# First mixture of experts: blocks beyond the second nested one inside the other, expert 0's third block without a condition, its redo inside the innermost condition

## The chip, the core and the metric

The kernel runs on one core of a Trainium2 chip. The metric is the device time of one execution in microseconds (us). Below, PE is TensorE, ACT ScalarE, DVE VectorE, POOL GpSimd and SP SyncE, which here only issues DMAs. Each engine has a sequencer of its own that reads its instruction stream, branches included.

## The reference, cut to what matters

Attention over chunks of 64 tokens gives 2304 rows of 512 values. A gate sends each row to one of 8 experts (the first mixture); a second mixture, dense over all 8 experts, follows and takes most of the time. The change is in the first mixture.

```python
logits = x @ w_gate
expert_idx = np.argmax(logits, axis=1)
...
h = np.maximum(np.einsum('ecd,edf->ecf', disp, w1), 0.0)
y = np.einsum('ecf,efd->ecd', h, w2)
...
out[i] = gate_w[i] * y[expert_idx[i], pos[i]]
```

With the inputs of the reference the experts 0 to 7 get 512, 128, 466, 384, 174, 128, 320 and 192 rows. This decides which conditional blocks run.

## The kernel before

Every matrix product is made of float16 high and low parts, so a product of weights and rows takes three matmul passes. For each expert of the first mixture the function `blocks` computes rows in blocks of 128: the first product (lines L346 for matmuls, ACT L351 and DVE L352 for what leaves PSUM as `hh` and `hl`), then for each 128 rows the second product `y` (L855, 24 matmuls of 512 columns), its scaling (ACT L860 and L866, DVE L867 and L873) and two writes to DRAM issued by SP (L870, L875).

The order of instructions on each engine is the order in which the code is written. Per expert it is: the first 256 rows always ("main"), with the weights of the next expert split into halves (`w_split`, L241 to L250) and statistics of the weights after those (L170, L172) written between its parts; then the rest under conditions on `rc`, the expert's row count, which every engine loads into a register (L909). `If(rc > 256)` is L992, `If(rc > 384)` is L993, and `If(rc > 512)` is L995. Above 384, rows 256 to 511 are computed as one block of 256; between 257 and 384 an `Else` computes a single block of 128; above 512 a loop (L996) takes further blocks.

So experts 0 and 2 run the block of 256, experts 3 and 6 the `Else`, and experts 1, 4, 5 and 7 skip everything from L992.

Expert 0 begins before routing is complete: its first 256 rows are taken when only a part of the rows has been routed. `e_count` holds how many rows expert 0 had by then. If these were at most 255, its first two blocks must be done again with the full list: that is the redo, L1010, behind a load of `e_count` (L1009). Here the count is 256, so the redo is skipped. `prep` is a list of statistics and one weight split that expert 0's conditional part carries; `later` is the list of loads of expert 3's weights, which SP issues (L159) after it.

PSUM is handed out in turn by name: "p" has three banks, "y" two, "c" two. Main takes "p" for first products and "y" for `y`; the conditional part takes "c" for both.

## Time and profile before

| what | value |
|---|---|
| device time, median of 3 runs | 1786.7 us (1784.45 to 1787.1) |
| the profiled execution, its own time | 1790.8 us |
| its span, first to last instruction | 1789.1 us |
| PE busy | 1704.3 us, 95% of the span |
| DVE, ACT, POOL busy | 67%, 54%, 41% |
| mean granted PE clock | 0.982 |
| first mixture, from expert 0's first matmul to the last row written | about 137 to 419 us of the span |

PE is busy nearly all the time, so what counts is where PE stands still, and why. In a timeline row, the bracket at the end gives the idle time before it and what ended it: an engine with its line, "PEq" for PE's own sequencer, or "issue" where nothing in the records explains the wait. Records whose engine ends in q are a sequencer's; COMPARE_BRANCH is a branch, with the time that it took.

### The profile page before, as it was taken

What the parts mean: (1) busy time and instruction counts of PE and PEld (TensorE: products, weight loads), DVE (VectorE), ACT (ScalarE), POOL (GpSimd) and SP (SyncE); (2) the same over time, 40 slices, a digit from 0 to 9 for tenths busy, and PEclk for the clock granted to TensorE, in tenths of its full rate; (3) what the DMA queues carried; (4) which work ended last, traced back from release to release, by engine and by line L of the source; (5) the groups of instructions that cost most, each with busy time, mean ns of one, the idle gap of its engine ahead of it and who ended that gap; (6) DMA issues with size and microseconds to landing.
All of it is one profiled execution on the core that took longest, in us unless ns stands there. A gap on an engine that the chain in (4) does not pass through costs nothing.

```text
span 1789.1 us, 33018 instructions
## 1 busy us (share of the span) xinstructions
PE 1704.3 (95%) x13011; PEld 1233.6 (69%) x13011; DVE 1196.4 (67%) x2347; ACT 958.8 (54%) x1814; POOL 731.4 (41%) x754
## 2 busy tenths in 40 slices
PE   7879899898999999999999999999999999999995
PEld 6766557565555477777777777777777777777774
DVE  4896556755467766686677667677766786676652
ACT  7866456665345455665365445555643665453440
POOL 1355435551121335453355245453534553443432
PEclk9989899999999999999999999999999999999998
DMA  9756678953524222332324224223323141231200
GB/s 236 205 168 174 181 194 177 234 131 97 145 65 168 104 104 83 110 137 76 130 63 171 95 77 161 97 100 109 128 86 130 62 171 71 101 125 63 97 37 36
DMA packets 140908, 219.22 MB, mean 123 GB/s; under 512 B 62880, under 2 KB 81392, under 8 KB 140720
## 3 DMA queue, kind: packets, MB, share of 16 engines
q1 hardware_dynamic: 133728, 198.92, 35.7%
q0 software_dynamic: 5360, 17.24, 3.4%
q8 instruction: 117, 1.92, 0.5%
q14 instruction: 71, 0.58, 0.1%
q10 hardware_dynamic: 1632, 0.56, 0.1%
HBM read 167.56 MB, written 41.91 MB: 117 GB/s over the span
## 4 chain that ended last, share of the span: by engine, by line
PE 68%; DVE 5%; ACT 2%; DMA 1%; issue 0%; POOLq 0%; ACTq 0%; DVEq 0%
PE p_m L1228 35%; PE p_m L1316 28%; PE p_m L1360 5%; DVE wall L292 3%; DVE acc L1295 1%; ACT wall L291 1%; DMA out_dram<-acc,rk 1%; DVE el L1236 0%; PE p_m L1116 0%; ACT eh L1233 0%; DMA x_d<-row 0%; DVE tq L1243 0%; ACT tq L1268 0%; DVE tq L1246 0%; DVE wall L250 0%
## 5 line engine op out<-in xcount | busy, mean ns | idle before, releaser
L1228 PE MATMUL p_m<-x,wall 128*128 128x384 f16 x4032 | 667.5, 326 | 6.9 <-ACT tq L1268 4.1
L1316 PE MATMUL p_m<-wall,eh 128*128 128x256 f16 x3528 | 580.3, 273 | 0.0
L1228 PEld LDWEIGHTS <-wall 128*128 128x128 f16 x4032 | 394.2, 98 | 264.7 <-issue 10.3
L1240 POOL TENSOR_TENSOR el<-tq,eh 128x384 f16<-128x384 f32 x336 | 344.5, 1053 | 558.4 <-ACT eh L1233 558.0
L1316 PE MATMUL p_m<-wall,el 128*128 128x256 f16 x1764 | 480.8, 273 | 0.3 <-DVE el L1236 0.3
L1233 ACT ACTIVATE eh<-tq 128x384 f16<-128x384 f32 x540 | 273.9, 522 | 190.5 <-DVE tq L1246 101.9
L1316 PEld LDWEIGHTS <-eh 128*128 128x128 f16 x3528 | 344.3, 98 | 44.3
L1295 DVE SCALAR_TENSOR_TENSOR acc<-p_m,cf,acc 128x256 f32<-128x256 f32 (+1 forms) x378 | 175.0, 520 | 128.1 <-PE p_m L1316 128.1
L1243 DVE TENSOR_TENSOR tq<-p_m,tq 128x384 f32<-128x384 f32 x288 | 158.3, 555 | 129.6 <-PE p_m L1228 128.6
L1316 PEld LDWEIGHTS <-el 128*128 128x128 f16 x1764 | 172.6, 98 | 20.6 <-DVE el L1236 0.6
L1236 DVE SCALAR_TENSOR_TENSOR el<-tq,eh 128x384 f16<-128x384 f32 x204 | 175.5, 862 | 10.0 <-ACT eh L1233 8.6
L1246 DVE SCALAR_TENSOR_TENSOR tq<-tq 128x384 f32<-128x384 f32 x252 | 133.0, 553 | 2.9
L346 PEld LDWEIGHTS <-wall 128*128 128x128 f16 x1152 | 107.2, 101 | 39.9 <-issue 23.1
L1268 ACT COPY tq<-p_m 128x384 f32<-128x384 f32 x96 | 45.6, 475 | 112.4 <-PE p_m L1228 110.1
L346 PE MATMUL p_p<-xT,wall 128*128 128x256 f16 x672 | 78.1, 277 | 15.7 <-PEq L1010 8.0
L1360 PE MATMUL p_m<-wall,eh 128*128 128x512 f16 x288 | 85.6, 379 | 0.0
L270 POOL TENSOR_TENSOR tq<-stb 128x256 f32<-128x256 f32 x56 | 48.9, 874 | 81.9 <-DVE wsumsq L186 58.9
L1281 ACT ACTIVATE tq<-tq 128x384 f32<-128x384 f32 x84 | 43.9, 523 | 70.1 <-DVE tq L1243 70.1
L291 ACT ACTIVATE wall<-stb,wsb 128x256 f16<-128x256 f32 (+1 forms) x56 | 31.3, 606 | 86.3 <-DMA wb_d<-wall 60.8
L242 POOL TENSOR_SCALAR stb<-stb,wsb 128x1024 f32<-128x1024 f32 x16 | 51.6, 3225 | 59.4 <-DVE tq L1243 47.2
L270 POOL TENSOR_TENSOR tq<-sta 128x256 f32<-128x256 f32 x56 | 45.0, 803 | 72.8 <-DVE wall L292 43.4
L292 DVE SCALAR_TENSOR_TENSOR wall<-stb,wsb,wall 128x256 f16<-128x256 f32 (+1 forms) x56 | 38.1, 689 | 50.2 <-ACT wall L291 47.4
(276 smaller groups left out, 2145.4 us busy)
## 6 DMA issues: line engine op xcount, KB each, us to landing
x<-xt_d SPq DMA_DIRECT2D x147, 384.0 KB
sta<-in_moe_w_dram SPq DMA_DIRECT2D x18, 1024.0 KB
stb<-in_moe_w_dram SPq DMA_DIRECT2D x18, 1024.0 KB
wb_d<-wall SPq DMA_DIRECT2D x20, 896.0 KB
wall<-wb_d SPq DMA_DIRECT2D x20, 896.0 KB
sta<-in_moe_w_dram SPq DMA_DIRECT2D x28, 512.0 KB
stb<-in_moe_w_dram SPq DMA_DIRECT2D x28, 512.0 KB
xt_d<-x SPq DMA_DIRECT2D x21, 384.0 KB
```

The costliest lines, as they stand in the source:

```text
L270: nc.gpsimd.tensor_tensor(out=at(o), in0=at(u), in1=at(v), op=op)
L292: nc.vector.scalar_tensor_tensor(out=o[:, cs, 1], in0=src, scalar=m.s, in1=o[:, cs, 0], op0=ALU.mult, op1=ALU.subtract)
L346: nc.tensor.matmul(p[:, f4, :], lhsT=w[:, kk, f * 128:(f + 1) * 128], rhs=xT[:, lo + kk, 0:W], start=(n == 0), stop=(n == 3 * KD - 1))
L1228: nc.tensor.matmul(p, lhsT=wt[:, w, lw, kk, :], rhs=xt[:, lx, kk, :], start=first and n == 0, stop=n == 5, skip_group_check=not first)
L1233: nc.scalar.activation(out=hs[op][0][:, q, :], in_=src, func=AF.Relu if op in (A11, A12, A22) or plain else AF.Copy)
L1236: nc.vector.scalar_tensor_tensor(out=hs[op][1][:, q, :], in0=src, scalar=0.0, in1=hs[op][0][:, q, :], op0=ALU.max, op1=ALU.subtract)
L1240: nc.gpsimd.tensor_tensor(out=hs[op][1][:, q, :], in0=src, in1=hs[op][0][:, q, :], op=ALU.subtract)
L1243: nc.vector.tensor_tensor(out=o, in0=a, in1=b, op=ALU.add)
L1246: nc.vector.scalar_tensor_tensor(out=o, in0=a, scalar=0.0, in1=b, op0=ALU.max, op1=op)
L1295: nc.vector.scalar_tensor_tensor(out=acc[:, j, cols], in0=y, scalar=coefs[x][:, j:j + 1], in1=acc[:, j, cols], op0=ALU.mult, op1=ALU.add)
L1316: nc.tensor.matmul(bk.t[:, cols], lhsT=hs[op][lh][:, q, t * 128:(t + 1) * 128], rhs=b.q[q][:, w, lw, :], start=m in (1, 5) and q == 0 and ...
L1360: nc.tensor.matmul(y.t, lhsT=h[:, kk % 4, c * 128:(c + 1) * 128], rhs=w[:, kk, :], start=(n == 0), stop=(n == 3 * KF - 1))
```

## The change

Expert 0's third block (`further(2)`) is computed without a condition, and holds `prep` in three parts where it was four. For the other experts it stands under `If(rc > 256)`, now L1017. Inside stands `If(rc > 384)`, L1020, with the fourth block (`further(3)`), and inside that `If(rc > 512)`, L1022, with `rest`: the loop, and for expert 0 the redo (L1008). So rows 256 to 511 are two single blocks, and there is no `Else`. For expert 0 `rc` is a new number, `e_more`: its count, or 2304 if the redo is due, so that the redo is reached. `y` in the nested blocks takes the banks "y"; what `rest` computes takes "c".

```diff
         def counted():
             nc.vector.tensor_copy(e_count, p_tab[:, 256:258])
+            nc.vector.tensor_scalar(out=e_redo, in0=p_tab[:, 256:257], scalar1=255.0, scalar2=float(N),
+                                    op0=ALU.is_le, op1=ALU.mult)
...
         nc.vector.tensor_copy(reg_i[:, 0:2 * E], p_tab[:, 256:256 + 2 * E])
+        nc.vector.tensor_tensor(out=e_more, in0=e_redo, in1=p_tab[:, 256:257], op=ALU.max)
...
-                y = bank("y", [128, DM])
+                y = in_turn(y_bank, [128, DM], F32, "p_y")
...
-                rc = count()
+                rc = count(True)
...
-            with tc.If(rc > 256) as more:
-                with tc.If(rc > 384) as cmp:
-                    blocks(x, (late_t, late_r), 2, ranks(2), [prep[0:4], prep[4:8], prep[8:], [], [], []])
+            def further(t, sites=()):
+                blocks(x, (late_t[:, :, (t - 2) * 128:(t - 1) * 128], late_r[t - 2:t - 1]), 1, lambda _: rank(t), sites)
+
+            def rest():
+                c = count() if x == 0 else rc
+                with tc.If(c > 512) if x == 0 else nullcontext():
+                    with tc.For_i(4, (c + 127) // 128, 1) as t:
...
+                if x == 0:
+                    with tc.If(nc.values_load(e_count[0:1, 0:1], min_val=0, max_val=N) <= 255):
+                        for t in range(2):
+                            blocks(x, turn(gather(tokens(0, t), "xgl", 1), "xTl", "c"), 1, lambda _, t=t: ranks(0)(t), y_bank="c")
...
+            if x == 0:
+                further(2, [prep[0:4], prep[4:], []])
+            with tc.If(rc > 256) if x > 0 else nullcontext():
+                if x > 0:
+                    further(2)
+                with tc.If(rc > 384):
+                    further(3)
                     with tc.If(rc > 512):
...
-                with cmp.Else():
-                    blocks(x, (late_t, late_r[:1]), 1, ranks(2), [prep[0:4], prep[4:], []])
+                        rest()
             if x == 0:
-                with more.Else():
-                    for f in prep:
-                        f()
-                known = nc.values_load(e_count[0:1, 0:1], min_val=0, max_val=N)
-                with tc.If(known <= 255):
-                    for t in range(2):
-                        blocks(x, turn(gather(tokens(0, t), "xgl", 1), "xTl", "c"), 1, lambda _, t=t: ranks(0)(t))
                 for f in later:
                     f()
```

On PE, this is what stands at the end of expert 0 before the change: from the last matmul of the conditional part to the first matmul of expert 1. The left-out rows are the two redo blocks.

```order
L855 MATMUL p_y<-wall,hl 128x512
L993 UNCONDITIONAL_BRANCH
L992 UNCONDITIONAL_BRANCH
L1009 TENSOR_LOAD e_count
L1010 COMPARE_AND_BRANCH
L331 LDWEIGHTS xg
...
L855 MATMUL p_y<-wall,hl 128x512
L1010 UNCONDITIONAL_BRANCH x2
L346 LDWEIGHTS wall
```

The same place on PE after the change, from the last matmul of the fourth block; the left-out rows are the loop's block and the two redo blocks.

```order
L860 MATMUL p_y<-wall,hl 128x512
L1022 COMPARE_AND_BRANCH
L914 TENSOR_LOAD reg_i
L1002 COMPARE_AND_BRANCH
...
L1008 TENSOR_LOAD e_count
L1008 COMPARE_AND_BRANCH
...
L860 MATMUL p_y<-wall,hl 128x512
L1008 UNCONDITIONAL_BRANCH x2
L1022 UNCONDITIONAL_BRANCH
L1020 UNCONDITIONAL_BRANCH
L348 LDWEIGHTS wall
```

The load of `e_count` and the branch on it no longer stand between the last block and expert 1: they lie in what L1022 jumps over, which holds the loop's block (258 instructions on PE) and the redo (512).

On DVE, expert 0's third and fourth block before the change, from the register load on (`stb`, `wsb` belong to the weights of the next experts):

```order
L909 TENSOR_LOAD reg_i
L992 COMPARE_AND_BRANCH
L993 COMPARE_AND_BRANCH
L352 SCALAR_TENSOR_TENSOR hl<-p_p,hh 128x512
L172 TENSOR_REDUCE wmxb<-stb_2263 128x1 x2
L352 SCALAR_TENSOR_TENSOR hl<-p_p,hh 128x512
L172 TENSOR_REDUCE wmxb<-stb_2263 128x1 x2
L352 SCALAR_TENSOR_TENSOR hl<-p_p,hh 128x512
L250 SCALAR_TENSOR_TENSOR w_3_2226<-stb_1830,wsb,w_2_2225 128x1024
L352 SCALAR_TENSOR_TENSOR hl<-p_p,hh 128x512
L89 TENSOR_SCALAR x2h<-ssq_2571 128x1
```

And after the change:

```order
L914 TENSOR_LOAD e_more
L354 SCALAR_TENSOR_TENSOR hl<-p_p,hh 128x4x128
L172 TENSOR_REDUCE wmxb<-stb_2267 128x1 x2
L354 SCALAR_TENSOR_TENSOR hl<-p_p,hh 128x4x128
L172 TENSOR_REDUCE wmxb<-stb_2267 128x1 x2
L250 SCALAR_TENSOR_TENSOR w_3_2230<-stb_1832,wsb,w_2_2229 128x1024
L89 TENSOR_SCALAR x2h<-ssq_2565 128x1
L872 SCALAR_TENSOR_TENSOR row_2573<-p_y,x2s,row_2573 128x2x256
L878 SCALAR_TENSOR_TENSOR rkt<-xg,x2i,iw 128x1
L1020 COMPARE_AND_BRANCH
L354 SCALAR_TENSOR_TENSOR hl<-p_p,hh 128x4x128 x2
```

All statistics and the split of `prep` now lie in the third block; the fourth, behind L1020, carries none.

## Rows read from the trace of the kernel before

**Rows 1.** The page, busy time and share of the span by engine.

```profile
PE 1704.3 (95%) x13011; PEld 1233.6 (69%) x13011; DVE 1196.4 (67%) x2347; ACT 958.8 (54%) x1814; POOL 731.4 (41%) x754
```

**Rows 2.** The chain that ended last, its first piece after 120 us: start, us, what.

```profile
415.08 4.23 DMA x_d<-row
```

**Rows 3.** PE's timeline, expert 0's conditional part and the start of expert 1.

```profile
162.55 0.60 PE L346 MATMUL p_p<-xTc,wall 128*128 128x256 f16 x4 [0.87 <-ACT xTc L333]
163.58 10.20 PE L346 MATMUL p_p<-xTc,wall 128*128 128x256 f16 x92 [0.43 <-DVE x2h L89]
174.44 0.59 PE L855 MATMUL p_y<-wall,hh 128*128 128x512 f16 x2 [0.66 <-DVE hl L352]
...
193.01 5.12 PE L346 MATMUL p_p<-xT,wall 128*128 128x256 f16 x24 [8.05 <-PEq L1010]
```

**Rows 4.** Stretches around that gap: busy us by engine, PE clock, DMA share, GB/s.

```profile
188.00:193.00 5.00, 0.00 (x0) 0.10 (x1) 0.00 (x0) 0.00 (x0) 2.26 (x4) 0.50 0.57 162
193.00:198.00 5.00, 4.99 (x26) 3.48 (x25) 0.00 (x0) 0.00 (x0) 0.00 (x0) 0.52 0.42 32
```

**Rows 5.** PE's sequencer there: ns min/median/max, first and last start us.

```profile
L995 PEldq COMPARE_BRANCH  x2: 343/496/648, 180.9 to 185.2; - x2
L995 PEldq EVENT_SEMAPHORE  x1: 51/51/51, 185.0 to 185.0; - x1
L1009 PEldq TENSOR_LOAD <-e_count x1: 318/318/318, 185.9 to 185.9; - x1
L1010 PEldq COMPARE_BRANCH  x1: 5997/5997/5997, 186.3 to 186.3; - x1
```

**Rows 6.** PE's sequencer at L992 and L993 of experts 1, 3, 4, 5, 6.

```profile
L992 PEldq COMPARE_BRANCH  x1: 3821/3821/3821, 213.8 to 213.8; - x1
L992 PEldq COMPARE_BRANCH  x1: 73/73/73, 286.0 to 286.0; - x1
L993 PEldq COMPARE_BRANCH  x1: 3720/3720/3720, 286.2 to 286.2; - x1
L992 PEldq COMPARE_BRANCH  x1: 3566/3566/3566, 320.3 to 320.3; - x1
L992 PEldq COMPARE_BRANCH  x1: 6147/6147/6147, 345.9 to 345.9; - x1
L993 PEldq COMPARE_BRANCH  x1: 3738/3738/3738, 371.3 to 371.3; - x1
```

**Rows 7.** PE's timeline after expert 0: where it stood still.

```profile
218.57 2.78 PE L346 MATMUL p_p<-xT,wall 128*128 128x256 f16 x24 [0.71 <-issue]
...
249.08 7.03 PE L346 MATMUL p_p<-xTc,wall 128*128 128x256 f16 x48 [2.17 <-DVE hl L352]
267.54 2.78 PE L346 MATMUL p_p<-xT,wall 128*128 128x256 f16 x24 [1.07 <-PEq L995]
...
290.05 5.52 PE L346 MATMUL p_p<-xTc,wall 128*128 128x128 f16 x96
297.29 0.60 PE L855 MATMUL p_y<-w,hh 128*128 128x512 f16 x2 [1.08 <-issue]
...
324.99 2.78 PE L346 MATMUL p_p<-xT,wall 128*128 128x256 f16 x24 [0.65 <-PEq L992]
332.14 6.51 PE L346 MATMUL p_p<-xT,wall 128*128 128x256 f16 x58 [2.47 <-issue]
352.68 2.78 PE L346 MATMUL p_p<-xT,wall 128*128 128x256 f16 x24 [2.78 <-DMA sta<-in_moe_w_dram]
380.35 3.41 PE L346 MATMUL p_p<-xTc,wall 128*128 128x128 f16 x58 [2.89 <-issue]
```

**Rows 8.** PE's timeline: the matmul behind the copy of `reg_i`.

```profile
149.84 0.35 PE L179 MATMUL p_sum<-wmxa,ones 128*128 128x4 f32 x2 [0.38 <-DVE reg_i L780]
```

**Rows 9.** DVE's timeline, a wait for weights in expert 2's main part.

```profile
240.86 1.22 DVE L172 TENSOR_REDUCE wmxb<-stb 128x1 f32<-128x1024 f32 x1 [0.71 <-DMA stb<-in_moe_w_dram]
```

**Rows 10.** SP's timeline: the loads that follow expert 0's conditional part.

```profile
195.05 1.91 SPq L159 DMA_DIRECT2D sta<-in_moe_w_dram  x4
```

## The prediction

> **What bounds the kernel now.** I read the busy times first: PE works 95% of the span [rows 1], so a change must either shorten PE's work or close gaps in it. Then the chain that ended last: its first piece after 120 us is the write of the last rows of the first mixture, at 415.08 us [rows 2], and all that follows, the second mixture, hangs on it. What the first mixture saves before that write, the end of the kernel gets. So PE's timeline of the first mixture is the view that counts. In it the largest gap by far is 8.05 us at the end of expert 0, from 184.96 to 193.01, ended by PE's own sequencer at L1010 [rows 3].

> The sequencer's records say how it comes about. At 180.9 us, 4 us before PE finished its queued matmuls, the sequencer reached L995 and jumped over the loop; the semaphore of that skipped branch was set at 185.0, when PE had drained; only then came the load of `e_count` (318 ns) and the branch L1010, 5997 ns [rows 5]. The jump over the redo thus stood behind an empty queue and was paid in full. [...]

> Other long jumps cost the sequencer as much and PE less. At experts 1, 3, 4, 5 and 6 they took 3.57 to 6.15 us [rows 6], but they began while matmuls were queued: at expert 1 the jump began at 213.8 and PE worked on until 217.86, idle 0.71 us [rows 7]. Some are followed by a second stop a few dozen matmuls later, marked "issue". Counted with it, PE lost 0.71 at expert 1, 1.08 at 3, 0.65 + 2.47 = 3.12 at 4, 2.78 at 5 (there the jump of 6147 ns ended at 352.05, so I read the DMA named in that row as a bystander) and 2.89 at 6 [rows 6, 7]. Their mean is 10.58 / 5 = 2.1 us. That is my price for a long jump with a full queue; its bounds are 0.7 and 3.1.

> **The change part by part.**

> *Expert 0's end.* The load and branch on `e_count` go into the part that L1022 jumps over. L1022 comes straight behind the last matmul of `y`, as L995 did, so it starts some 4 us before PE is done. It is long (the loop's block and the redo, longer than L1010's), so 2.1 takes the place of 8.05: -5.9 us (bounds -7.3 and -4.9).

> *The clock.* The slow start of expert 1 cost 5.12 - 2.78 = 2.34. It falls away unless the shorter gap also lowers the clock. Of four gaps between 2.1 and 2.9 us, at 249, 332, 353 and 380 us, one was followed by slow matmuls: 48 in 7.03 us where 92 took 10.20, so 5.3 would do, 1.7 lost [rows 3, 7]. A quarter of about 2 is 0.5: -1.8 us (bounds -2.3 and 0).

> [...]

> *Expert 0's blocks.* One block of 256 becomes two of 128. In PE's own time this is nothing: 96 matmuls of 128 columns took 5.52 us [rows 7], two such sets 11.04, against 96 of 256 columns at the rate of 92 in 10.20 [rows 3], 10.6: +0.4. Waits before: 0.43 for the second half of `xTc`, 0.66 for the last `hl` [rows 3]. In a single block the first product uses two banks once, and `y` starts with the four slices that left PSUM while the second bank was filled, so the 0.66 should go, and of the 0.87 and 0.43 about half, as only the first 128 columns of `xTc` are needed: -1.3 at best, -0.9 taken. Sum -0.5 (bounds -0.9 and +0.4). `prep` is hidden behind PE's second product as before; should DVE's statistics run late, the fourth block has none in its way.

> *Expert 2.* The same split, +0.4 in matmuls. Its wait of 2.17 for `hl` stays: DVE is late there by statistics that wait for weights (0.71 of it seen directly [rows 9]), and `y` needs that `hl` as the third bank did. Its L995 becomes L1022, with one branch more that is not taken (73 ns [rows 6]). Its end cost 1.07; if its short jump (343 to 648 ns at expert 0 [rows 5]) turned long it would cost 2.1. I take +0.6 for all (bounds +0.1 and +2.4).

> *Experts 3 and 6.* The long jump moves from ahead of the third block (L993 to `Else`) to behind it (L1020 over the fourth block and the loop). It is hidden by the same kind of queue, `y` of the block in place of `y` of main. 2 x 2.1 in place of 1.08 + 2.89: +0.2 (bounds -2.6 and +2.3).

> *Experts 1, 4 and 5.* The same jump over almost the same amount of code, but the code has moved, so the second stops may fall elsewhere: 3 x 2.1 in place of 6.61: -0.3 (bounds -4.5 and +2.8).

> *The new DVE operations.* `e_more` stands right behind the copy of `reg_i`, which a matmul waited for, 0.38 us [rows 8]; a second small operation there adds at most its own time. +0.1 (bounds 0 and +0.2). `e_redo` lies in the attention part, DVE having room.

> *Other queues.* SP issued expert 3's loads at 195.05 us [rows 10], held back by expert 0's end; they come earlier with it. POOL, ACT and DVE each lose a register load and a branch, off PE's path.

> The sum: -5.9 - 1.8 - 0.5 + 0.6 + 0.2 - 0.3 + 0.1 = -7.6 us. It is made on the profiled execution, 1790.8 us long (a span of 1789.1), which is 4.1 us above the median of 1786.7; I set it against the median: **1779.1 us**, 0.43% less.

> **The rivals.**

> *The refill takes it back.* Each of the six long jumps that lead into first-mixture work (experts 0, 1, 3, 4, 5, 6) could cost the dearest price, 3.1, the second stop being laid anew at every one. That is 18.7 in place of 8.05 + 10.58 = 18.6, and with one slow-clock stretch of 2 us the 2.34 is gone too: only the -0.5 and +0.7 of the blocks are left, so about 1787, no change. For it: three of the five had a second stop. Against it: two had none. With half the second stops, 1782 to 1785 comes out. [...]

> *Weights late.* PE comes 7 us earlier, but the loads hang on DMA. DVE waited 0.71 for them [rows 9], and a delay there stops PE through `hl`. Expert 3's loads also start earlier [rows 10], and in the gap DMA was busy for only 0.57 of the time [rows 4]. If half is lost: 1783.

> *Slower.* The jump behind a block is not hidden. If the semaphores of the nested branches must wait for PE to drain before the jump, as L1010's did behind L995's [rows 5], then L1022 costs 8 as now, and experts 3 and 6 pay 6 to 8 each at their ends in place of 4 together: +8 to +12, 1795 to 1799. It decides from the point where the branch record starts after the last matmul's end and not 4 us ahead. Against it: L995, L992 all began ahead.

> *Cheaper.* No second stop at all: six jumps at 0.7 to 2.8, gaining 4 us more: 1775.

> **How the numbers follow.** The forecast 0.54, the refill 0.22 or the weights 0.10 taking back a part or all, slower 0.07, cheaper 0.07. The three runs before lie within 2.7 us, 0.15%; 0.2%, or 3.6 us, is about what such a measurement tells from no change. Faster, below 1783.1: 0.54 + 0.07 and 0.15 of the 0.32 that take back, 0.76. Within: the other 0.17. Slower: 0.07. The range reaches down to the cheaper case and up over most of the refill: 1775 to 1785.5.

> **What would show it.** Right: no gap over 3 us at expert 0's end; L1022's branch record 3.5 to 6 us long and starting about 4 us before the last `y` ends; a granted clock of 1.00 at expert 1's start; the last write some 7 us before 415. Wrong: a branch record that starts after PE drained; new "issue" stops early in experts 1 and 2; DVE's waits for `stb` longer than 0.71 and PE waiting for `hl`.

## The result, and the profile after

The change made the kernel slower: 1799.1 us (median of 9 runs, 1790.2 to 1802.6) against 1785.7 (9 runs of the kernel before beside it), a ratio of the means of 1.0065 with a 95% interval of 1.0044 to 1.0085 (all ratios below are made so, each against runs of the kernel before beside it). The forecast was 1779.1. The trace taken first was of the shortest of the nine runs (1790.16 us), so a second execution, of 1799.73 us, was traced as well and is the one read here. Set against the trace of before, itself of a long run (1790.8 us), it shows 8.9 us more span; the medians differ by 13.4.

PE's busy time is what it was [rows 1], and so is the whole second mixture; the loss lies ahead of the last write of the first mixture [rows 2]. The page and the chain that ended last, usual execution after:

```profile
PE 1704.2 (95%) x13203; PEld 1232.6 (69%) x13203; DVE 1199.6 (67%) x2349; ACT 959.3 (53%) x1814; POOL 731.5 (41%) x754
```

```profile
423.94 4.57 DMA x_d<-row
```

The best view of it is the table of stretches, cut at the first matmul of each expert. Columns: start and end; length, PE busy us and instructions, PE clock, DMA share, GB/s. The rows are experts 0 to 7. Before:

```profile
136.70:193.01 56.31, 45.93 (x326) 0.92 0.64 171
193.01:218.57 25.56, 24.75 (x165) 0.91 0.70 197
218.57:267.54 48.97, 45.04 (x308) 0.97 0.72 196
267.54:301.84 34.30, 33.12 (x285) 1.00 0.79 177
301.84:324.99 23.15, 22.41 (x165) 1.00 0.84 190
324.99:352.68 27.69, 22.43 (x164) 1.00 0.93 245
352.68:388.78 36.10, 33.12 (x285) 1.00 0.64 158
388.78:415.08 26.30, 23.02 (x175) 1.00 0.31 82
```

After, the usual execution:

```profile
135.45:187.89 52.44, 44.84 (x423) 1.00 0.69 179
187.89:212.53 24.64, 23.83 (x165) 0.94 0.81 215
212.53:264.75 52.22, 46.55 (x404) 0.93 0.70 184
264.75:307.06 42.31, 32.96 (x285) 0.92 0.77 176
307.06:331.76 24.70, 23.98 (x164) 0.93 0.57 122
331.76:359.72 27.96, 23.88 (x164) 0.94 0.96 228
359.72:396.35 36.63, 32.96 (x284) 0.99 0.58 167
396.35:423.94 27.59, 24.15 (x171) 0.95 0.32 79
```

Row by row, after less before: -3.9 (expert 0), -0.9, +3.3 (expert 2), +8.0 (expert 3), +1.6, +0.3, +0.5, +1.3: together +10.1. Expert 0 began 1.3 us earlier; 10.1 - 1.3 is the 8.9 us by which the last write came later, and by which the span grew. So expert 0's end did gain, and experts 2 and 3 lost three times as much.

Where PE stood still in the usual execution after (to be held against [rows 3, 7]):

```profile
187.89 4.20 PE L348 MATMUL p_p<-xT,wall 128*128 128x256 f16 x24 [5.04 <-PEq L914]
212.53 2.67 PE L348 MATMUL p_p<-xT,wall 128*128 128x256 f16 x23 [0.71 <-PEq L1017]
218.97 0.40 PE L348 MATMUL p_p<-xT,wall 128*128 128x256 f16 x1 [3.77 <-issue]
264.75 2.78 PE L348 MATMUL p_p<-xT,wall 128*128 128x256 f16 x24 [0.88 <-PEq L1022]
307.06 4.34 PE L348 MATMUL p_p<-xT,wall 128*128 128x256 f16 x24 [9.25 <-PEq L1020]
```

And PE's sequencer at its branches there (against [rows 5, 6]; min/median/max ns, start us):

```profile
L1022 PEldq COMPARE_BRANCH  x1: 7820/7820/7820, 179.1 to 179.1; - x1
L1017 PEldq COMPARE_BRANCH  x1: 3602/3602/3602, 207.8 to 207.8; - x1
L1020 PEldq COMPARE_BRANCH  x1: 12004/12004/12004, 294.1 to 294.1; - x1
L1020 PEldq COMPARE_BRANCH  x1: 5412/5412/5412, 389.5 to 389.5; - x1
```

The reader is to see two things. Expert 3's jump, now behind its third block, lasted 12.0 us where the one ahead of that block had taken 3.7 [rows 6]; PE was idle for 9.25 of them, and expert 4's first 24 matmuls ran slowly after it (4.34 us in place of 2.78). And expert 2 has a second stop, 3.77 us, 23 matmuls in.

Why a branch lasts 12 us shows in the DMA queues, where the page lists queues of kind "instruction". In the first trace of the changed kernel (packets, MB, share):

```profile
q8 instruction: 118, 1.93, 0.4%
```

That is 16.4 KB a packet. The 26406 matmuls and weight loads that the page counts on PE make 224 a packet, and all of PE's branches of over 2 us ended shortly behind a q8 packet (below), so I take q8 for PE's instruction queue; that is an estimate. In the usual execution, expert 3's jump began at 294.1. For the next 8 us no instruction packet came; the queues in 294 to 302 (packets, MB, share of 16 engines):

```profile
q1 hardware_dynamic: 387, 0.93, 51.3%
q0 software_dynamic: 78, 0.27, 37.0%
```

and in 302 to 304, where it came (a packet is counted where its record starts; this one lasted from 303.79 to 304.74, and the jump ended at 306.14):

```profile
q1 hardware_dynamic: 136, 0.34, 45.3%
q0 software_dynamic: 26, 0.10, 24.7%
q8 instruction: 1, 0.02, 2.9%
q14 instruction: 2, 0.02, 1.9%
```

q0 holds POOL's gathers (`xg<-xs_d`), q1 all that SP issues: weight loads, written rows, transposes. Every long jump and every second stop looked at has such a q8 packet. In the six of the table PE's sequencer goes on 1.3 to 1.5 us after the end of the packet's record, 2.2 to 2.5 us after its start, whether it came at once or late (where the expectations below say 2.5 us from the landing, they count from the start):

| stop | began | q8 packet's record | ended | record's end to stop's end |
|---|---|---|---|---|
| after, shortest run: expert 4's jump | 315.97 | 316.97 to 317.93 | 319.29 | 1.36 |
| same: expert 1's jump, under weight loads | 202.71 | 206.80 to 207.70 | 209.22 | 1.52 |
| after, usual run: expert 0's jump | 179.12 | 184.53 to 185.61 | 186.94 | 1.33 |
| same: second stop in expert 2 | 215.20 | 216.74 to 217.68 | 218.97 | 1.29 |
| same: expert 3's jump | 294.14 | 303.79 to 304.74 | 306.14 | 1.40 |
| before: expert 5's jump | 345.87 | 349.52 to 350.61 | 352.02 | 1.41 |

All sixteen traces together have 119 branches of PE that took over 2 us; 113 of them ended 1.2 to 1.6 us behind the end of a q8 record, the other six 0.8 to 1.8 us.

So a long jump costs some 2.4 us from the start of its packet's record (2.3 to 2.9 in 14 of the 15 branches of over 2 us in the trace of before and that of the shortest run after), plus the wait until that start: about 1.0 us where the queues are quiet (jumps of 3.3 to 3.8 us), 3.7 to 9.7 us in the other jumps of the table. The record itself can grow too: it took 3.6 us for L1010 of before, from 187.40 to 191.00.

### The profile page after: what moved, and what is told of

Read it like the earlier page. It is cut to its first block, busy times and chain, and to the rows that moved or that the text cites. A ratio compares the mean times of both kernels' runs of the same rounds, so it can differ in the third digit from the quotient of the medians.

```text
span 1788.4 us, 33391 instructions
## 1 busy us (share of the span) xinstructions
PE 1706.2 (95%) x13203; PEld 1237.4 (69%) x13203; DVE 1195.2 (67%) x2349; ACT 959.7 (54%) x1814; POOL 730.2 (41%) x754
## 4 chain that ended last, share of the span: by engine, by line
PE 67%; DVE 6%; ACT 2%; DMA 1%; issue 1%; POOLq 0%; ACTq 0%; DVEq 0%
PE p_m L1240 35%; PE p_m L1328 27%; PE p_m L1372 5%; DVE wall L292 3%; ACT wall L291 1%; DVE acc L1307 1%; DMA out_dram<-acc,rk 1%; DVE el L1248 0%; PE p_m L1128 0%; DMA wb_d<-wall 0%; ACT eh L1245 0%; DVE tq L1255 0%; DMA x_d<-row 0%; ACT tq L1280 0%; DVE tq L1258 0%
## 5 line engine op out<-in xcount | busy, mean ns | idle before, releaser
L1240 PEld LDWEIGHTS <-wall 128*128 128x128 f16 x4032 | 394.1, 98 | 265.3 <-issue 10.6
L348 PE MATMUL p_p<-xT,wall 128*128 128x256 f16 x672 | 82.7, 287 | 18.8 <-PEq L1020 5.8
```

The lines of the kernel that those rows point to most:

```text
L348: nc.tensor.matmul(p[:, f4, :], lhsT=w[:, kk, f * 128:(f + 1) * 128], rhs=xT[:, lo + kk, 0:W], start=(n == 0), stop=(n == 3 * KD - 1))
L1240: nc.tensor.matmul(p, lhsT=wt[:, w, lw, kk, :], rhs=xt[:, lx, kk, :], start=first and n == 0, stop=n == 5, skip_group_check=not first)
```

## The experiments

Fourteen runs were made. Theory 1, held first: expert 0's gain is real, and the other experts' jumps now begin while weight loads fill the queues. Theory 2, the rival: the single blocks and their banks cost time themselves. Theories 3 and 4 grew out of the traces and are told where they come in.

**The two halves of the change.** Expert 0 as changed with experts 1 to 7 in the old nesting, and the reverse:

```diff
-            with tc.If(rc > 256) if x > 0 else nullcontext():
-                if x > 0:
-                    further(2)
+            if x == 0:
                 with tc.If(rc > 384):
...
+            else:
+                with tc.If(rc > 256) as more:
+                    with tc.If(rc > 384) as cmp:
+                        blocks(x, (late_t, late_r), 2, ranks(2), y_bank="c")
```

> Expert 0 as changed, experts 1 to 7 as before. Theory 1 (expert 0's gain is real, and what was lost is the jumps of the other experts, which now begin while weight loads fill the DMA queues): some 7 us faster than before, 1777 to 1781, with a gap under 3 us at expert 0's end. Theory 2 (the single blocks and their banks cost time by themselves, in expert 0 too): no faster than before, 1785 or more.

> Expert 0 as before, experts 1 to 7 as changed. Theory 1: slower than the whole change by expert 0's 7 us, so 1.0 to 1.2% above before, 1803 to 1808, with long branch records (5 to 8 us) behind the third blocks of experts 3 and 6. Theory 2: 0.3 to 0.6% above before, and the loss in matmuls or in waits for banks, not in branch records.

Expert 0 alone: 1783.6 us, 0.9967 (0.9949 to 0.9986), so faster by 0.33%, though short of the 1777 to 1781 expected. Experts 1 to 7 alone: 1806.4, 1.0102 (1.0078 to 1.0125). The gap at expert 0's end was 1.87 us in the first and 8.30 in the second:

```profile
187.86 2.78 PE L348 MATMUL p_p<-xT,wall 128*128 128x256 f16 x24 [1.87 <-PEq L914]
```

The gain at expert 0 is real, and the loss is all in the others. This does not yet tell the theories apart.

**The changed kernel again** (the usual execution read above), and the loads behind the conditional part:

> The changed kernel once more, for a second trace: the one at hand is of its fastest run of nine (1790.2 us; the median is 1799.1). Theory 1: the extra time of a usual run lies in branch records and the stops behind them, in the same experts 1, 3 and 6. Theory 2: it lies elsewhere.

The usual execution's span is 9.6 us longer than the shortest run's (1798.0 against 1788.4). Its gaps were longer by 3.4 us at expert 0's end, 3.2 at expert 2's second stop and 3.5 at expert 3's jump, and 2.4 shorter at expert 1's. So the extra time lies in branches and the stops behind them, as expected, but in experts 0, 2 and 3, not 1, 3 and 6.

```diff
-                sites += [later[:2] + stats if x != E - 2 else load(E, "b", 0, 1, 2, 3) + stats, later[2:]]
+                sites += [stats if x != E - 2 else load(E, "b", 0, 1, 2, 3) + stats, []]
...
-            if x == 0:
-                for f in later:
-                    f()
+            for f in later:
+                f()
```

> The changed kernel, but the loads of the first matrix three experts on are issued behind the conditional part of experts 1 to 5, not between the parts of main. Theory 1: expert 3's jump finds empty DMA queues and takes 3.3 to 3.9 us in place of 8.3, so 5 us or more faster than the changed kernel; expert 6's, whose loads stay, keeps 5 us or more. Theory 2: as the changed kernel, within 2 us.

1791.2 us, 1.0024 (1.0010 to 1.0039): about 8 us of the loss came back. Expert 1's and 4's jumps were short (3.4 us), but expert 3's still took 7.5 us and its gap 4.43, where 3.3 to 3.9 had been expected; from 290 to 292 the times of q0's packets added up to 147% of the 16 engines' time, and no other queue started a packet. Theory 1 is half right: weight loads matter, and gathers too. From here Theory 3 says that a jump waits for its packet behind any DMA.

**Experts 3 and 6 back in the old nesting**, the rest as changed; **gathers moved** in the kernel with loads behind; a **copy added** that nobody reads; and **expert 0 alone with loads behind**:

```diff
+            if x in (3, 6):
+                with tc.If(rc > 256) as more:
+                    with tc.If(rc > 384) as cmp:
...
                 nxt.append(turn(late_cur, "xTc", "p"))
+                if x == 4:
+                    nxt.append(rows_ahead())
...
+                if x == 4:
+                    for i in range(2):
+                        nc.scalar.dma_start(out=spare_d[i * 384:(i + 1) * 384, :], in_=w1[i][0:384, :])
```

> The changed kernel with experts 3 and 6 alone back in the old nesting (both conditional blocks under one branch, the single block under its Else, so that the long jump stands ahead of the third block again). Theory 3 (a long jump on PE lasts some 2.5 us from the landing of the 16 KB packet of the instruction queue that it waits for; that packet waits behind whatever the DMA queues carry, and behind the third block of expert 3 they carry POOL's gathers and weight loads): expert 3's record falls from 8.3 to 12.0 us to about 3.5, expert 6's from 5.5 to about 3.5, and the time from 1799 to 1785 to 1790. Theory 2 (single blocks and their banks cost time themselves, at expert 2 too): no more than 4 us come back, 1795 or more.

> The changed kernel with the first-matrix loads behind the conditional part, as in the run before, and two sets of POOL's gathers moved: those issued around expert 0's jump go behind its conditional part, those issued around expert 3's jump go behind expert 4's first product. Nothing else changes. Theory 3: the instruction packet of both jumps is served within about 1 us, so expert 0's record falls from 8.6 to about 4.5 us and expert 3's from 7.5 to about 3.5, PE's gap at expert 3 from 4.4 us to about 1; the time about 1783 against 1791. Rival (the length of the jump is set by the code jumped over, not by the traffic): both records stay at 7 to 9 us.

> The changed kernel with a copy of 3 MB from memory to memory added (two DMAs that ACT issues behind expert 4's first product; nobody reads it). Expert 4's jump was the quietest: 3.3 to 3.8 us in all six kernels traced so far, its instruction packet landing 0.75 to 1.0 us after it began. Theory 3: the record grows to 5 us or more, the packet landing later by as much as the record grows and the jump ending 2.5 us behind it. Rival (length set by the code): 3.3 to 3.8 us as ever.

> Expert 0 as changed, experts 1 to 7 in the old nesting, and the first-matrix loads behind each conditional part. Theory 3: expert 1's jump, 7.4 us under loads with expert 0 alone changed, falls to about 3.5 and its gap of 4.0 us and slow clock go, so that the time is 1777 to 1781, below expert 0 alone (1783.6 in its runs). Rival (loads behind the conditional part only move the collision on to the second stops and make weights late): 1784 or more.

The copy settles the mechanism (in one trace, with PE's code where it was): DMA traffic alone lengthens the jump. Expert 4's jump, 3.3 to 3.8 us in every other kernel but the two in which transfers had been moved behind it (5.3 and 6.3), took 8.5 us and left a gap of 5.15; no q8 packet started from 326 to 332, while the copy (q10) ran:

```profile
L1021 PEldq COMPARE_BRANCH  x1: 8532/8532/8532, 326.0 to 326.0; - x1
```

```profile
q10 hardware_dynamic: 41, 1.03, 50.6%
q1 hardware_dynamic: 134, 0.25, 13.0%
q0 software_dynamic: 54, 0.20, 11.4%
q14 instruction: 1, 0.01, 0.8%
```

Its record lasted from 332.09 to 333.06, and the jump ended at 334.55, 1.5 us behind it. The window in which it started:

```profile
q0 software_dynamic: 9, 0.03, 33.2%
q8 instruction: 1, 0.02, 24.2%
```

Of the other three, all expectations failed on the time. With the gathers moved, expert 0's jump fell to 3.3 us and its gap to 0.94, and expert 3's gap from 4.43 to 2.36 (its jump from 7.5 to 5.4, not the 3.5 expected), but the total was 1794.3 (1.0053, 1.0037 to 1.0069): expert 1's jump was now caught (6.3 us), a second stop of 3.62 came in expert 5, and in expert 0's fourth block, from 173.4 to 178.9, PE stood still seven times, marked "issue", 4.3 us together, with a granted clock of 0.50 in the 4.4 us from 179.6 on. What held PE there is not known. Expert 0 alone with loads behind gave 1794.5 (1.0047, 1.0030 to 1.0063): expert 1's jump became short (3.9 us), those of 3 and 4 long (6.8 and 6.3). Here, moving a transfer away from one jump moved it onto another. And with experts 3 and 6 in the old nesting their jumps were indeed 3.3 and 3.6 us, but the time was 1797.7 (1.0075, 1.0053 to 1.0097), as Theory 2 had it. PE's timeline of that kernel points away from Theory 2: four second stops, all "issue", 23, 43, 11 and 31 matmuls behind a jump's landing.

```profile
218.04 0.28 PE L348 MATMUL p_p<-xT,wall 128*128 128x256 f16 x1 [3.67 <-issue]
290.48 4.75 PE L348 MATMUL p_p<-xTc,wall 128*128 128x128 f16 x53 [4.02 <-issue]
330.10 2.96 PE L348 MATMUL p_p<-xT,wall 128*128 128x256 f16 x13 [5.34 <-issue]
383.87 6.58 PE L348 MATMUL p_p<-xTc,wall 128*128 128x128 f16 x65 [4.73 <-issue]
```

Each ended 1.3 to 1.4 us after the end of a q8 record too (289.04 for the second, 328.81 for the third); the fourth's record had taken 4.65 us. The longest second stop of all traces stands in the kernel with experts 1 to 7 alone changed, right at the landing in expert 2; its expert 5 has another, of 5.53 us:

```profile
222.96 5.28 PE L348 MATMUL p_p<-xT,wall 128*128 128x256 f16 x24 [7.56 <-SPq L1031]
```

Counting PE's instructions in program order, a matmul with its weight load as two and a float32 matmul as four (the count under which the places fit), the twelve second stops of these two kernels, of before, of the changed kernel and of expert 0 alone lie from 2 instructions ahead of to 17 behind a multiple of 256. So the places fit blocks of 256 instructions. The second stops seen, all within 96 matmuls of a landing, cost 0.6 to 7.6 us.

**The code shifted, nothing that runs changed.** Theory 4: what decides the second stops is how far behind the landing the block ends. Matmuls that never run, in the part behind `If(rc > 512)`, put every landing just behind such a multiple of 256:

```diff
+            def pad():
+                p = bank_tile(turns["c"][0], [128, 512], F32, "p_y")
+                for _ in range((75, 89, 89, 57, 95, 88, 57, 94)[x]):
+                    nc.tensor.matmul(p[:, 0:128], lhsT=id16, rhs=id16)
...
             def rest():
+                pad()
```

> The changed kernel with matmuls that never run added to the part behind the last nested branch of each expert (75 to 90 of them, reached only by experts with more than 512 tokens), so that the code of the next expert begins just behind a boundary of 256 PE instructions. Nothing that runs is changed. Theory 4 (behind a long jump PE has only the block of instructions it landed in; where that block ends a few dozen matmuls later, PE stops a second time, until 2.5 us after the landing of the next packet, which DMA traffic delays): the second stops 23 matmuls into expert 2 (0.6 to 3.8 us) and 31 matmuls into expert 5 (2.2 to 2.6 us) go, the jump of expert 3 stays at 8 to 12 us: 1791 to 1795 against 1799. Rival (the traffic alone decides, not where the code lies): the stops stay, 1797 to 1801.

> The kernel with experts 3 and 6 back in the old nesting, and matmuls that never run added so that the target of each long jump lies just behind a boundary of 256 PE instructions. Nothing that runs is changed. Without them four second stops were seen, 23 matmuls into expert 2 (3.7 us), 43 into expert 3's third block (4.0), 11 into expert 5 (5.3) and 31 into expert 6's third block (4.7). Theory 4: all four go, 17.7 us with some 3 of slow clock, and the time falls from 1797.7 to 1778 to 1784. Theory 2 (single blocks and their banks cost time themselves): no more than 3 us come back.

> Expert 0 as changed, experts 1 to 7 in the old nesting, and never-run matmuls that put the target of each long jump just behind a boundary of 256 PE instructions. Theory 4: the one second stop of expert 0 alone changed (3.8 us, 52 matmuls into expert 6's third block) goes, the jumps under weight loads (experts 1 and 5, 7.4 and 6.4 us) stay: 1779 to 1782, against 1783.6. Rival (that kernel's lead is traffic alone): 1783 or more.

> The kernel before with never-run matmuls that put the targets of the long jumps of experts 0 to 7 just behind a boundary of 256 PE instructions; nothing that runs is changed. Theory 4: the second stops of expert 5 (2.5 us, 40 matmuls in) and of expert 6's third block (2.9) go: 1780 to 1783 against 1786, and the gap of 8 us at expert 0's end stays. Set against expert 0 alone aligned, it gives what the change of expert 0 is worth where the code lies alike: 3 to 6 us less with the change. Rival: 1785 or more, stops where they were.

No second stop of over 0.7 us is left behind a jump in any of the four. The changed kernel fell to 1792.4 us (1.0022, 1.0006 to 1.0038), the one with 3 and 6 in the old nesting by 22 us to **1775.7** (0.9935, 0.9916 to 0.9954), more than expected and the fastest of all kernels that keep the branches. Its expert 3 passes from main to the third block without a gap:

```profile
278.97 0.38 PE L860 MATMUL p_y<-w,hl 128*128 128x512 f16 x1
279.19 5.02 PE L348 MATMUL p_p<-xTc,wall 128*128 128x128 f16 x87
```

These two differ only in the nesting of experts 3 and 6, with it the bank of that block's `y`, and the padding, and landings lie alike, so 16.8 us is what the moved jump costs, the luck of two schedules included. The trace of the aligned changed kernel has over half of it in one row, ended by the jump:

```profile
298.55 1.87 PE L348 MATMUL p_p<-xT,wall 128*128 128x256 f16 x8 [8.94 <-PEq L1026]
```

The other two missed: expert 0 alone 1785.2 (0.9984, 0.9969 to 0.9999), before 1790.2 (1.0010, 0.9998 to 1.0022), each without its second stops but with a new gap at expert 2's end, which had cost 1.07 [rows 7]:

```profile
261.63 5.28 PE L348 MATMUL p_p<-xT,wall 128*128 128x256 f16 x24 [5.05 <-DMA rk_d<-rkt]
```

In the old nesting, expert 2 leaves by two jumps, over the loop and over the `Else`. Both records were now long (3.75 and 4.36 us; 0.33 and 0.38 in the trace of before). The first jump skips 258 instructions without the padding and 386 with it. Whether that made it long is not shown: in the shortest run of the changed kernel, which has no padding, expert 2's jump over 258 instructions took 3.39 us (L1022, at 252.2). Set against each other, the two kernels give expert 0's change 5.0 us, as expected.

**What else delays expert 3, and what all jumps cost.** The aligned changed kernel with only the gathers around expert 3's jump moved (as above), and the changed kernel with the branches on counts decided when the program is built; the latter leaves out the loop over further blocks and the redo, which these inputs never reach.

> The changed kernel with never-run matmuls as in the aligned run, and with one set of POOL's gathers moved: those issued around expert 3's jump go behind expert 4's first product. The weight loads stay where they are, and PE's code does not move. Theory 3 (expert 3's jump behind its third block waits for a packet that POOL's gathers hold up): its record falls from 11.2 us to 5 to 7, PE's gap there from 8.9 to 2 to 4, and the time from 1792.4 to 1784 to 1788. Rival (the weight loads alone hold it up): the record stays over 9 us and the time over 1790.

> The changed kernel with the branches on the counts of experts 0 to 7 decided when the program is built, for the counts of these inputs; the loop over further blocks and the redo are left out. Every block that ran still runs, in the same order. It shows what all jumps together cost. Theory 3 and 4 (what the changed kernel lost, and most of what the first mixture still stands idle, are fetches of instructions): no gap over 1 us at an expert's end and no slow clock behind one, 1766 to 1772. Theory 2 (single blocks and their banks cost time themselves): 1780 or more.

With the gathers away, expert 3's jump took 7.6 us in place of 11.2, its gap 4.77 in place of 8.94; until its packet came at 292.83 only q1 (weight loads, written rows) was moving. Record and gap fell by less than expected, and the time, 1791.6 (1.0022, 0.9999 to 1.0045), did not follow: a new gap of 3.71 us, waiting for DVE, stands at 352.21 in expert 5. Without the branches: 1764.2 us (0.9860, 0.9827 to 0.9892), 35 us less than the changed kernel with the same blocks in the same banks. At expert 4's start, where the 9.25 us stood, PE's matmuls now follow each other:

```profile
288.01 0.38 PE L860 MATMUL p_y<-w,hl 128*128 128x512 f16 x1
288.23 2.02 PE L348 MATMUL p_p<-xT,wall 128*128 128x256 f16 x17
```

That rules Theory 2 out as the main cause: with the same blocks and banks the loss is gone. Whether single blocks cost a microsecond or two is not shown; for that the old blocks would have to be run without branches too. One gap stays at expert 0's end, 3.12 us, and waits for data:

```profile
185.82 2.45 PE L348 MATMUL p_p<-xT,wall 128*128 128x256 f16 x15 [3.12 <-DMA xT<-xg]
```

## Why the prediction was wrong

**The step that failed** is the one on experts 3 and 6: "It is hidden by the same kind of queue, `y` of the block in place of `y` of main. 2 x 2.1 in place of 1.08 + 2.89: +0.2 (bounds -2.6 and +2.3)." The queue of matmuls was the same, the transfers were not. Ahead of the third block the DMA queues left room for the packet: 3.3 to 3.8 us in all kernels but the one with loads moved there. Behind it POOL's gathers, weight loads and written rows are in flight: 7.5 to 12.0 us at expert 3 (5.4 where loads and gathers were both moved away), and at expert 6, 4.7 to 6.1. In the usual execution the rows of experts 3 and 4 (its slow start) lost 9.6 us, those of 6 and 7 1.8; the aligned pair gives 16.8. The price of 2.1 with bounds 0.7 and 3.1 came from jumps of before, whose idle time had hidden that their length is a wait for a DMA packet. One row of before held the hint: expert 5's jump of 6147 ns ended beside a weight load [rows 7], and I "read the DMA named in that row as a bystander".

**Expert 0's end**, -5.9: right in kind, too large. L1022 did start about 4 us ahead of PE's end (at 179.1, PE idle from 182.85), but lasted 4.4 to 8.6 us, since gathers run there too (3.3 us once they were moved). In eleven traces with the new end and those gathers in place the gap was 1.7 to 5.9, mean 3.9; in three with the old, 7.8 to 8.3. So -4.2.

**The clock**, -1.8: half. In the 4.2 us behind the gap of 5.04 us the granted clock was 0.65 (0.52 in the 5 us behind the gap of before [rows 4]), and expert 1's first 24 matmuls took 4.20 us in place of 5.12 [rows 3]: -0.9.

**Expert 0's blocks**, -0.5: of the table's -3.9 for expert 0 the gap makes 3.0 (8.05 to 5.04); -0.9 is left for the blocks and all else, not seen apart.

**Expert 2**, +0.6: the wait for `hl` that I kept was gone, with either half of the change alone too (with experts 1 to 7 alone changed, behind the stop of 7.56 us), worth 2.2 and a slow stretch; its end cost 0.88, not 2.1. The second stop 23 matmuls in took it all back: +3.3 in the row.

**Experts 1, 4 and 5**, -0.3: their jumps were much as before (3.6, 3.3 and 4.7 us against 3.8, 3.6 and 6.1). The second stops did "fall elsewhere", 23 and 31 matmuls into experts 2 and 5. But I priced them by the mean of before, without asking how late the packet would be there: PE stood 3.8 us at the one and 2.6 at the other.

**The rivals.** "Slower" had the right sign and place, with another mechanism: the jump began ahead of the drain and was long all the same. That its 1795 to 1799 came so near the 1799.1 is luck. "The refill takes it back" named the second stops, which came, and had too low a cap. "Weights late" showed one of its signs, a DVE wait of 1.12 us for `stb` at 171.25 in expert 0, but PE had no gap of over 0.5 us in that part, so it is not where the time went. "Cheaper" found no support.

**What stays open**: why L1020 behind expert 6's third block took 4.7 to 6.1 us in all eight traces that have it, with two q8 records that begin 1.8 to 3.1 us apart in each; how much of expert 3's wait is weight loads and how much written rows; and whether a late packet waits in a queue or for the memory, since the runs show only that it comes late while other transfers run.

## What to carry to other kernels

In the first mixture of before and of the changed kernel a branch of PE took 0.07 to 0.65 us or 3.3 to 12.0; each long one ended behind a packet of the instruction queue, and that packet came late while the kernel's own DMAs ran (3.3 us became 8.5 beside the copy): price such a jump by what the DMA queues carry at that moment, not by a jump elsewhere. Put such jumps where transfers are quiet, or decide them ahead of time, and when a change moves code, look where the next multiple of 256 instructions lies behind each landing: that alone was worth 22 us here in one kernel, and nothing in the two in which another jump was long with the padding.
